# When and in how many issues q is asked for in a fused attention and feed-forward kernel

## The chip, the cores and the metric

The kernel runs on one core of a Trainium2 chip. The metric is the device time of one execution in microseconds (us), lower is better. Engines are called PE (TensorE, matrix products), DVE (VectorE), ACT (ScalarE), POOL (GpSimd) and SP (SyncE, which here only issues DMAs). A DMA is issued by an engine's queue (in this kernel SP's, POOL's and, at the start and the end, ACT's).

## The reference

```python
# q, k, v: (8, 8, 576, 64)   batch, heads, sequence, head size
kv  = np.einsum('bhsd,bhse->bhde', k, v)
out = np.einsum('bhsd,bhde->bhse', q, kv)
rms = np.sqrt(np.mean(out * out, axis=-1, keepdims=True) + 1e-06)
attn = out / rms * g_norm
# (B,H,S,D) -> (B*S, H*D) = (4608, 512)
x = attn.transpose(0, 2, 1, 3).reshape(B * S, H * D)
h = x @ w_in                     # (512, 2048)
r = np.maximum(h, 0.0)
y = (s * (r * r) + b) @ w_out    # (2048, 512)
```

All data is float32; the changes of this study touch only how q is brought into the chip.

## The kernel before

The 4608 rows of x are cut into 36 chunks of 128 rows, and four chunks make a unit: nine units. For each unit the kernel computes attention of its four chunks, then the first product (x @ w_in), the squared relu, and the second product (@ w_out). The attention of unit u + 1 is laid beside the products of unit u, two chunks at a time, so that PE goes from one product to the next. The large products are done in the manner of Strassen (seven products in place of eight, with sums on DVE); names such as x1, z2, x6, y7, x5, x3, y4 are the seven partial products, and the letter is the PSUM tag they use.

The order on each engine is the order in which the program calls its functions (`tc.manual_schedule()`); waits on semaphores are added where one instruction needs another's data or buffer.

**How q comes in.** `load_q(c)` (L132) fills one tile q_sb of 128 x 1024 for chunks c and c + 1. The pool has two buffers (`qp`, L77), so the tile of chunk 8 takes the buffer of chunk 4, and its DMAs wait until the last reader of that one is done (`norm`, L559). From chunk 4 on the tile is put together from pieces: `parts` (L119) says which columns j of which batch a chunk has, and for each piece of n neighbouring columns there are 16 DMAs, one for each of 8 heads and 2 halves of 32 in the head. Chunks 4 and 5 have two single columns (n = 1) and one piece of 6; chunks 6 and 7 one piece of 8; chunks 8 and 9 two pieces of 4; chunks 10 and 11 one piece of 8. `loads(u, i)` (L1599) issues them all on POOL's queue; i is the half of the unit. At most eight DMAs of POOL are under way at a time: each issue waits for the one eight before it.

**What reads q.** `attention_of_two(c)` (L490) gives the steps, in this order: `turn` (DVE transpose, L514, into qT), `product` (PE, L526, into y_ps), `back` (DVE, L538), `square` (ACT, L545), `row_sum` (L549, L553), `norm` (DVE, L557 and L559), `turn_x` (DVE, L570), `scale` (ACT, L488). A is the first pair of chunks of the next unit, B the second. These steps are hung into the products by tables: `side_of` (L1571) for the second product of the first two units, by slot number, and `sides` (L1665) for the first product of later ones.

**The first unit.** It runs beside the conversion of the weights, which come as raw tiles of 1 MB (`load_w`, L177, on SP's queue, three buffers): each is worked over by ACT (`raw`, L217 and L222) and DVE (`convert`, L227 and L237), and then the next raw tile is asked for. `first_unit` (L1613) interleaves this with the plain first product, in slots n. When g_s1(0), a DVE sum, is done, POOL is let on by a tiny copy called begin, and asks for q of the second unit, chunks 4 to 7.

**The stores.** In the second product of unit 0 (`mm2(0)`) the partial products x3 (slots 10 and 11) and y4 (slots 12 and 13) each end with `store` (L1187): two DMAs on POOL's queue. The steps of `side_of` for slot n follow the product of slot n. After the last slot the second unit (u = 1) starts; it asks for chunks 8 to 11 first of all, and then for its weights by SP (`pump`, L1009; the ring w_sb).

Of the kernel before, what the change touches and what calls it, by code (L numbers as in the profile page):

```python
# [16 lines left out]
def kernel(  # L17
# [39 lines left out]
    nc = tc.nc  # L57
    P = 128
    B, H, S, D = q.shape
# [59 lines left out]
    def parts(c):  # L119

        if c < 4:
            return [(0, c, 1), (0, 4 + c, 1)]
        if c == 4:
            return [(0, 8, 1), (0, 17, 1), (1, 0, 2)]
        g, i = divmod(c, R)
        if g == 0:
            return [(1, 4 * i - 18, 4)]
        if i == 4:
            return [(2 * g, 16, 2), (2 * g + 1, 0, 2)]
        return [(2 * g, 4 * i, 4)] if i < 4 else [(2 * g + 1, 4 * i - 18, 4)]  # L130

    def load_q(c, queues=(nc.sync, nc.sync), rest_on=nc.gpsimd):  # L132

        t = qp.tile([P, 2 * DM], FP32, name="q_sb", tag="q")
        q_tile[c] = t
        if c < 4:
            for i in range(2):
                q_in[c + i] = t[:, i * DM : i * DM + DM].rearrange("p (h d) -> p h d", h=H)  # L140
            for s, queue in enumerate(queues):
                for i in range(2):
                    b, j, _ = parts(c + i)[s]
                    queue.dma_start(
                        out=q_in[c + i][s * HB : s * HB + HB],
                        in_=q[b].rearrange("h (p j) d -> p j h d", j=R)[:, j],
                    )
            return []
        pieces, w = [], 0
        for b, j, n in parts(c) + parts(c + 1):  # L150
            if pieces and pieces[-1][1] == b and pieces[-1][2] + pieces[-1][3] == j:
                pieces[-1][3] += n
            else:
                pieces.append([w, b, j, n])
            w += n
        rest = []
        for w, b, j, n in pieces:
            src = q[b].rearrange("h (t j) d -> h t j d", j=JC)
            to = t.rearrange("p (a w d) -> p a w d", a=NP, d=32)
            for h in range(H):  # L160
                for a in range(2):
                    rows = slice(32 * (2 * (h % 2) + a), 32 * (2 * (h % 2) + a) + 32)
                    rest.append(
                        partial(
                            rest_on.dma_start,
                            out=to[rows, h // 2, w : w + n, :],
                            in_=src[h, :, j : j + n, a * 32 : a * 32 + 32],
                        )
                    )
        return rest  # L170
# [152 lines left out]
    for h in range(H):  # L323
        e = D // KC
        nc.gpsimd.dma_start(
            out=g_col[h * e : h * e + e, :], in_=g_norm.rearrange("(e c) -> e c", c=KC)
# [282 lines left out]
    ga, g_pair = {}, {}  # L609
# [901 lines left out]
    turn, take, product, square, root, norm, turn_x = zip(*(attention(c) for c in range(4)))  # L1511
# [59 lines left out]
    def side_of(A, B, sums, u):  # L1571

        if u == 0:
            return {
                6: [A["turn"], lambda: kv_product(1)],
                8: [A["product"], A["back"], A["square"]],
                9: [A["row_sum"], B["turn"]],
                10: [A["norm"], A["turn_x"], A["scale"], B["product"], B["back"], B["square"]],
                11: [B["row_sum"], B["norm"]],
                12: [B["turn_x"], B["scale"], lambda: [fn() for fn in sums_w_in(0)]],  # L1580
                13: [sums],
            }
        of_w_in = [
            partial(sums_of_w_in, *with_tags)
            for with_tags in zip(DEEP, ((5, 6), (7, 4), (5, 6)))
        ]
        return {
            0: [A["scale"]],
            1: [B["turn"]],
            4: [B["product"], B["back"], B["square"]],  # L1590
            5: [B["row_sum"]],
            6: [B["norm"], of_w_in[1]],
            8: [B["turn_x"], B["scale"], of_w_in[2]],
            11: [sums],
            13: [partial(loads, 3, 1)],
            3: [of_w_in[0]],
        }

    def loads(u, i):  # L1599

        if u < U:
            for load in load_q(4 * u + 2 * i):
                load()  # L1603
# [9 lines left out]
    def first_unit():  # L1613
        of_x = x_sums(0)
        of_w = []

        for n, slot in enumerate(slots0):
            if n == 11:
                of_w[1]()
            if n > 1:  # L1620
                out_of = slot()
                if out_of:
                    out_of()
                if n % 4 == 0:
                    g_s1(n // 4 - 1)
                if n == 4:
                    t = small("begin", 1)
                    nc.gpsimd.tensor_copy(out=t, in_=ga["s1", 0][:, 0, :1])
                    loads(1, 0)
                    loads(1, 1)  # L1630
            if 0 < n < 9:
                raw(n + 2)
                convert(n + 2)
            elif n == 0:
                continue
            elif n == 9:
                of_w += sums_w_in(3)
                of_w[0]()
            elif n == 10:
                of_x[0]()  # L1640
                raw(11)
                of_x[1]()
            if n < 11:
                scale_g()
            if n == 9:
                more(8)
        a = mm1(0, NS - 1)
        for fn in (
            a["x1"], scale_g, partial(convert, 11), partial(more, 9),
            a["z2"],  # L1650
            a["x6"], partial(raw, 12), scale_g, partial(g_s1, 2),
            a["y7"], partial(convert, 12),
            a["x5"], partial(raw, 13), scale_g, partial(more, 10), partial(more, 11),
        ):
            fn()
        return a
# [71 lines left out]
    for u in range(U):  # L1728
        A, B = pairs_of(u + 1) if u + 1 < U else (None, None)
        if u == 0:  # L1730
            last = first_unit()
            second = mm2(0)
        else:
            if u == 1:
                loads(2, 0)
                loads(2, 1)
            first, at_second = sides(u, A, B)
            if u > 1:
                run, last = mm1_deep(u)
                second = mm2(u, last, at_second)  # L1740
                run(lambda n: [fn() for fn in first.get(n, [])], second["early"])
                second["rest"]()
                continue
            steps = [mm1(u, s) for s in range(NS)]
            second = mm2(u)
        for s in range(NS if u > 0 else 0):
            a = steps[s]

            def at(n):
                for fn in first.get((s, n), []):  # L1750
                    fn()

            at(0)
            a["x1"]()
            if s:
                x3(steps[s - 1])
            a["z2"]()
            at(1)
            if s:
                y4(steps[s - 1])  # L1760
            a["x6"]()
            at(2)
            a["y7"]()
            at(3)
            a["x5"]()
        side = side_of(A, B, lambda: [fn() for fn in x_sums(u + 1)], u)
        for n, slot in enumerate(second):
            slot()
            if u == 0:
                if n == 0:  # L1770
                    convert(13)
                    load_kv(1, 0, convp, tag="raw", bufs=3)
                    for name in ("x3", "y4", "y4_square"):
                        last[name]()
                    raw(14)
                    scale_g()
                    last["x3_s1"]()
                elif n == 1:
                    convert(14)
                    load_kv(1, 1, convp, tag="raw", bufs=3)  # L1780
                    store_w2(1, 5)
                    raw(15)
                elif n == 2:
                    convert(15)
                    t2 = convp.tile([P, 4 * R * D], FP32, name="w_t2", tag="raw", bufs=3)
                    W2_AT[6] = t2[:, : FC // 2 * HN].rearrange("p (f n) -> p f n", n=HN)
                elif n == 4:
                    store_w2(3, 2)
                    sub_w_out(6, 3, 5)
                    store_w2(6)  # L1790
            if n == 0 and u > 0:
                x3(steps[-1])
                y4(steps[-1])
            for step in side.get(n, []):
                step()
        if u == 0:
            tc_late()
            pump()
# [30 lines left out]
```

## Time and profile before

| | |
|---|---|
| median of three plain runs | 911.52 us (911.5, 911.52, 914.25) |
| the profiled execution | 916.24 us, span 914.5 us |
| busy in the span | PE 898.0, DVE 670.1, ACT 355.5, POOL 276.8 us |
| issues of q on POOL (L1603) | 336, 188.3 us |
| issues of stores on POOL (L1191) | 120, 59.3 us |
| first unit's q issues, chunks 4 to 7 | 49.2 to 94.8 us, 64 issues |
| q issues of chunks 8 to 11 | 138.4 to 172.3 us, 48 issues |

The span is the part of the execution that the profile covers; times inside it count from its start. Most of an execution PE is busy, and what the other engines do matters only where PE, or a chain that ends in PE, waits for it. In the lines of a timeline the columns are the start, the duration of the group, the engine, the line of the program, the operation, the tile written and those read, the shape and the number of instructions; in brackets stands how long the engine was idle before the group, and what ended that. In the lines of waits stand the engine and line that waited, what it waited for, the sum in us, how many times, and the longest. The line with PEclk gives the granted clock of PE in 40 slices of the span, 9 for full speed.

### The profile page before, as it was taken

The page shows a single profiled execution, that of the slowest core. Times are in us where ns is not written, and L with a number is a line of the kernel's source. Part 1 is how long each engine was busy: PE and PEld are TensorE (multiplying, and loading weights), DVE is VectorE, ACT ScalarE, POOL GpSimd, SP SyncE. Part 2 cuts the span into 40 slices and gives each one's busy share as a digit, 9 for nine tenths or more (in the row PEclk, how much of TensorE's full clock was granted, in tenths as well). Part 3 has the DMA queues.
Part 4 walks back from the last instruction along what each step waited for, and adds up shares of the span by engine and source line. Part 5 has one row for each costly group of instructions (what it writes and reads, how often), then busy time and mean ns, then how long its engine had stood idle before and what let it go on. Part 6 is the DMA issues. An engine that isn't in the chain of part 4 may idle for free.

```text
span 914.5 us, 19293 instructions
## 1 busy us (share of the span) xinstructions
PE 898.0 (98%) x7494; PEld 824.3 (90%) x7494; DVE 670.1 (73%) x1236; ACT 355.5 (39%) x598; POOL 276.8 (30%) x523
## 2 busy tenths in 40 slices
PE   7999999899999999999999999999999999999998
PEld 6887888788889998999889998999899989999998
DVE  2889686477648886788678858785778768874686
ACT  2878124341146304640276016801581057204710
POOL 2068018303734142830274035603440200021000
PEclk9999999899999999999999999999999999999999
DMA  9686947329953895369725973498539812891286
GB/s 258 214 290 210 315 115 225 92 68 337 382 146 81 248 329 174 74 198 312 249 60 162 296 256 107 112 297 266 142 79 282 299 35 58 268 302 55 58 253 185
DMA packets 117579, 180.35 MB, mean 197 GB/s; under 512 B 25840, under 2 KB 43504, under 8 KB 117488
## 3 DMA queue, kind: packets, MB, share of 16 engines
q1 hardware_dynamic: 96272, 151.68, 53.3%
q0 software_dynamic: 17760, 25.20, 9.6%
q10 hardware_dynamic: 3456, 2.23, 1.0%
q8 instruction: 60, 0.98, 0.4%
q14 instruction: 31, 0.25, 0.1%
HBM read 153.36 MB, written 25.69 MB: 196 GB/s over the span
## 4 chain that ended last, share of the span: by engine, by line
PE 75%; DMA 8%; issue 7%; DVE 6%; POOL 3%; ACT 1%; ACTq 0%; DVEq 0%; POOLq 0%
PE x_ps L91 38%; PE y_ps L91 22%; PE z_ps L91 8%; PE sx_ps L91 4%; DMA q_sb<-in_q_dram 3%; PE y_ps L526 2%; DMA w<-sub 1%; POOL q_sb L1603 1%; DMA out_dram<-o 1%; DMA kv_sb<-in_v_dram 1%; POOL w L1091 1%; DMA w_raw<-in_moe_w_in_dram 1%; DMA w_raw<-in_moe_w_out_dram 1%; PE z_ps L358 1%; DVE xn L559 0%
## 5 line engine op out<-in xcount | busy, mean ns | idle before, releaser
L1603 POOL DMA_DIRECT2D q_sb<-in_q_dram x336 | 188.3, 568 | 143.8 <-ACT a L633 62.9
L1191 POOL DMA_DIRECT2D out_dram<-o x120 | 59.3, 501 | 314.6 <-issue 152.1
L91 PE MATMUL x_ps<-w_sb,sub 128*128 128x128 f32 x1176 | 148.8, 275 | 0.6 <-DVE r L242 0.6
L91 PEld LDWEIGHTS x_ps<-w_sb,sub 128*128 128x128 f32 x1176 | 139.7, 192 | 1.0 <-DVE r L242 0.9
L625 ACT ACTIVATE a<-a,b_col,s_col 128x512 f32<-128x512 f32 x144 | 116.2, 813 | 35.2 <-DVE a L628 28.0
L91 PE MATMUL x_ps<-xs,ws 128*128 128x256 f32 x528 | 125.7, 381 | 2.2 <-ACT r L699 2.2
L91 PE MATMUL y_ps<-xs,wb 128*128 128x256 f32 x528 | 126.4, 385 | 0.4 <-DVE a L242 0.4
L91 PEld LDWEIGHTS y_ps<-xs,wb 128*128 128x128 f32 x528 | 98.6, 192 | 14.1 <-DVE a L242 0.8
L91 PEld LDWEIGHTS x_ps<-xs,ws 128*128 128x128 f32 x528 | 97.0, 191 | 15.2 <-ACT r L699 3.4
L800 ACT COPY a<-x_ps 128x512 f32<-128x512 f32 x28 | 16.4, 584 | 216.2 <-PE x_ps L91 216.0
L91 PE MATMUL x_ps<-xT,wa 128*128 128x256 f32 x360 | 83.7, 381 | 0.1
L91 PEld LDWEIGHTS x_ps<-xT,wa 128*128 128x128 f32 x360 | 66.8, 190 | 10.4 <-issue 1.5
L242 DVE TENSOR_TENSOR r<-sx_ps,a 128x256 f32<-128x256 f32 x63 | 26.6, 422 | 61.7 <-PE sx_ps L91 61.5
L91 PE MATMUL x_ps<-w_sb,a 128*128 128x128 f32 (+1 forms) x432 | 64.9, 298 | 0.0
L91 PE MATMUL y_ps<-w_sb,a 128*128 128x128 f32 (+1 forms) x416 | 62.1, 295 | 0.0
L91 PEld LDWEIGHTS x_ps<-w_sb,a 128*128 128x128 f32 x432 | 58.9, 191 | 3.3 <-issue 0.4
L91 PEld LDWEIGHTS y_ps<-w_sb,a 128*128 128x128 f32 x416 | 56.1, 192 | 2.1
L242 DVE TENSOR_TENSOR a<-y_ps,r 128x512 f32<-128x512 f32 x38 | 26.1, 688 | 39.2 <-PE y_ps L91 31.2
L242 DVE TENSOR_TENSOR r<-x_ps,o 128x256 f32<-128x256 f32 (+1 forms) x84 | 29.7, 354 | 29.3 <-PE x_ps L91 28.6
L91 PE MATMUL y_ps<-w_sb,sub 128*128 128x128 f32 x392 | 49.5, 275 | 0.0
L245 DVE TENSOR_TENSOR a<-a,a 128x512 f32<-128x512 f32 x72 | 46.8, 684 | 0.4
L91 PE MATMUL z_ps<-w_sb,a 128*128 128x128 f32 (+1 forms) x352 | 46.8, 280 | 0.0
(182 smaller groups left out, 1516.0 us busy)
## 6 DMA issues: line engine op xcount, KB each, us to landing
w_sb<-w SPq DMA_DIRECT2D x385, 256.0 KB, 4.6
w_raw<-in_moe_w_in_dram SPq DMA_DIRECT2D x8, 1024.0 KB, 7.4
w_raw<-in_moe_w_out_dram SPq DMA_DIRECT2D x8, 1024.0 KB, 7.4
w_sb<-w SPq DMA_DIRECT2D x14, 512.0 KB, 8.9
w<-sub POOLq DMA_DIRECT2D x28, 256.0 KB, 6.2
out_dram<-o POOLq DMA_DIRECT2D x112, 64.0 KB, 4.0
w_sb<-in_k_dram SPq DMA_DIRECT2D x24, 288.0 KB, 5.0
w_sb<-in_v_dram SPq DMA_DIRECT2D x24, 288.0 KB, 5.3
```

The source lines that it names most:

```text
L91: nc.tensor.matmul(o, lhsT=lhsT, rhs=rhs, start=start, stop=stop, skip_group_check=True)
L242: nc.vector.tensor_tensor(out=o, in0=a, in1=b, op=ALU.add)
L245: nc.vector.tensor_tensor(out=o, in0=a, in1=b, op=ALU.subtract)
L358: nc.tensor.matmul(ps[r][(r ^ l) * HB : (r ^ l) * HB + HB, i, :], lhsT=kv[l][0][rows, j, :], rhs=kv[l][1][rows, j, :], start=(j == 0), sto ...
L526: nc.tensor.matmul(ps[l][32 * p : 32 * p + 32, r, lo:hi], lhsT=bd_kv[b % 2][rows, p, at : at + 32], rhs=st["qT"][rows, p, lo:hi], start=Tr ...
L625: nc.scalar.activation(t, t, AF.Identity, scale=s_col, bias=b_col)
L800: nc.scalar.copy(g_tile("a11", s), st["x", s])
L1091: nc.gpsimd.dma_start(out=w3_dram[i][:, m - 4], in_=t)
L1191: queues[s % 2].dma_start(out=view[b, jj, :, cols], in_=st[name, j][s * w : s * w + w, cols])
L1603: load()
```

## The change

Three things are changed. A piece of one single column (n = 1) takes one DMA for four heads in place of four DMAs: h runs over 2 in place of 8, and the DMA's pattern has the four heads h, h + 2, h + 4, h + 6 as a dimension. The copy begin waits for g_s1(1) in place of g_s1(0), and it, with q of the second unit, is put into slot 8 of the first product in place of slot 4. And `loads(2, 0)`, q of chunks 8 and 9, is put into slot 10 of the second product of the first unit, behind A's norm, in place of the start of the second unit; `loads(2, 1)` stays there.

```diff
-            for h in range(H):
+            for h in range(2 if n == 1 else H):
                 for a in range(2):
                     rows = slice(32 * (2 * (h % 2) + a), 32 * (2 * (h % 2) + a) + 32)
+                    d = slice(a * 32, a * 32 + 32)
+                    if n == 1:
+                        rest.append(
+                            partial(
+                                rest_on.dma_start,
+                                out=to[rows, :, w, :],
+                                in_=src[h::2, :, j, d].rearrange("h t d -> t h d"),
+                            )
+                        )
+                        continue
                     rest.append(
...
-                            in_=src[h, :, j : j + n, a * 32 : a * 32 + 32],
+                            in_=src[h, :, j : j + n, d],
...
-                10: [A["norm"], A["turn_x"], A["scale"], B["product"], B["back"], B["square"]],
+                10: [A["norm"], partial(loads, 2, 0), A["turn_x"], A["scale"], B["product"], B["back"], B["square"]],
...
-                if n == 4:
+                if n == 8:
                     t = small("begin", 1)
-                    nc.gpsimd.tensor_copy(out=t, in_=ga["s1", 0][:, 0, :1])
+                    nc.gpsimd.tensor_copy(out=t, in_=ga["s1", 1][:, 0, :1])
                     loads(1, 0)
                     loads(1, 1)
...
             if u == 1:
-                loads(2, 0)
                 loads(2, 1)
```

## The prediction, made before the changed kernel was run

> **What bounds the kernel now.** I read the page first, then the waits of TensorE, then TensorE's timeline around its longest wait, and last POOL's timeline and the DVE instruction that the wait names. From the page:
>
> ```profile
> PE 898.0 (98%) x7494; PEld 824.3 (90%) x7494; DVE 670.1 (73%) x1236; ACT 355.5 (39%) x598; POOL 276.8 (30%) x523
> PEclk9999999899999999999999999999999999999999
> ```
>
> TensorE (PE) is busy for 98% of the span, so a change that adds no matrix work can only win back PE's gaps, or create new ones. The granted clock dips once, in slice 7 (0-based; 160 to 183 us). The waits of PE are few:
>
> ```profile
> PE y_ps L526 <- DVE qT L514: 3.3, 1, 3.3
> PE x_ps L91 <- ACT r L699: 2.2, 2, 1.6
> PE kv_ps L358 <- DMA kv_sb<-in_v_dram: 1.7, 3, 1.0
> ```
>
> The first is one wait of 3.3 us in the second unit; the second is two waits, of 1.57 us (up to 72.14) and 0.62 us (up to 76.47), at the end of the first unit's first product. The third is the start of the kernel, which isn't touched. PE's timeline around the long wait:
>
> ```profile
> 162.21 1.89 PE L91 MATMUL z_ps<-xT,wa 128*128 128x256 f32 x8
> 167.38 1.96 PE L526 MATMUL y_ps<-qT,bd_kv 64*32 64x128 f32 x64 [3.28 <-DVE qT L514]
> 169.27 3.78 PE L91 MATMUL y_ps<-xs,wb 128*128 128x256 f32 x8
> 172.84 2.14 PE L91 MATMUL x_ps<-xs,ws 128*128 128x256 f32 x8
> 174.82 1.89 PE L91 MATMUL y_ps<-xs,wb 128*128 128x256 f32 x8
> ```
>
> Here the reader sees two losses: 3.28 us idle, and then eight matmuls that take 3.78 us where the same eight take 1.89 elsewhere: half clock. What PE waited for, and what POOL (which issues q) did before:
>
> ```profile
> 165.98 1.25 DVE L514 STREAM_TRANSPOSE qT<-q_sb 128x1024 f32<-128x1024 f32 x1 [5.00 <-DMA q_sb<-in_q_dram]
> ...
> 124.51 1.09 POOL L1191 DMA_DIRECT2D out_dram<-o  x2 [29.76 <-DVE inv L557]
> 129.19 1.05 POOL L1191 DMA_DIRECT2D out_dram<-o  x2 [3.58 <-DVE o L242]
> 133.37 1.06 POOL L1191 DMA_DIRECT2D out_dram<-o  x2 [3.13 <-DVE o L242]
> 137.36 1.05 POOL L1191 DMA_DIRECT2D out_dram<-o  x2 [2.93 <-DVE o L242]
> 138.40 3.29 POOL L1603 DMA_DIRECT2D q_sb<-in_q_dram  x6
> ...
> 144.00 3.79 POOL L1603 DMA_DIRECT2D q_sb<-in_q_dram  x7 [0.40 <-DMA out_dram<-o]
> 148.96 11.54 POOL L1603 DMA_DIRECT2D q_sb<-in_q_dram  x21 [1.17 <-DMA q_sb<-in_q_dram]
> ```
>
> DVE stood idle for 5.00 us for q of chunks 8 and 9. POOL could not ask for it before 138.40: the four pairs of stores stand ahead in its queue, and each waits for DVE's sums. The 32nd issue (6 + 1 + 7, then the 18th of the 21) falls at 148.96 + 17 x 0.55 = 158.3 us, and its data lands by 165.98, 7.7 us later, beside four 512 KB loads that SP issued from 155.8 to 157.8.
>
> [...] q's last pieces were slow (7.7 us against a median of 2.7 us for the 32 KB pieces) when SP's loads ran beside them. [...] In the trace POOL's q issues take 0.50 to 1.07 us from 49 to 95 us, where DVE converts weights, and 0.55 to 0.59 from 138 to 172; I keep the slower pace as a bound.
>
> **The change part by part.**
>
> (a) q of chunks 8 and 9 (32 issues) moves from behind all eight stores to behind the first two. These two go at 124.51. The buffer is that of chunks 4 and 5, whose last reader is A's norm on DVE (L559, 124.41 + 1.22 = 125.63), so the first issue comes at about 125.7 instead of 138.4, while SP's queue moves nothing (98 GB/s and a DMA share of 0.40 from 125 to 138). The pace before was (158.3 - 138.4)/32 = 0.62 us with its waits: 125.7 + 32 x 0.62 = 145.5 for the last one. With a landing of 2.7 to 7.7 us q is there at 148 to 153. PE needs the product at 162.21 + 1.73 = 163.94 (the pace of eight such matmuls), the transpose takes 1.25 us, so q is needed by 162.7: some 9 us of cover. The stall goes. What is late next: DVE is free at 160.98 (L628 ends), hence qT at 162.2, and the bd_kv copies end on ACT at 158.1; both are before 163.94, so nothing takes its place.
> Worth: without the stall the matmuls of L526 start at 164.0 and take 1.19 us (the x64 group at 115.39), the next eight 1.83, the next eight 1.73, so the group seen at 174.82 starts at 164.0 + 1.19 + 1.83 + 1.73 = 168.8. That is 6.0 us, of which 3.3 is idle and 2.7 is clock.
>
> (b) Behind the 32 issues: the six later stores (ready at 129, 133, 137) now go at about 145.5 to 148.7 (6 x 0.53). Who waits for them: the output tiles are next written in the second unit's second product, after 200. Then the 16 issues of chunks 10 and 11, from about 149 to 162 with waits on the stores' landing (5.4 us seen), instead of 158.9 to 172.3; their transpose comes beside the product that starts at 190. Cost nothing, the cover is over 30 us. SP is moved past nothing: its ring loads from 139.95 keep their place, and are first read at 190.36.
>
> (c) q of the second unit: POOL's start moves from g_s1(0) (48.5) to g_s1(1) on DVE (63.45 + 0.69 = 64.1). 32 issues of single columns (0.50 us each) become 8 of 32x4x32, a shape whose issues take 0.55 to 0.59 in (a); 16 + 16 others stay. 24 issues at 0.6 to 0.75 end at 79 to 82, all 40 at 88 to 94 (before: 94.8). Their transposes are at 108.17 and 121.81 on DVE: at least 13 us of cover with a 5 us landing.
> What it frees: from 49 to 64 the raw weight tiles fill the DMA engines (share 0.87, 290 GB/s). ACT waits 1.50 us for a raw tile until 59.44, and the chain of waits runs from that landing without a gap through ACT and DVE to PE at 76.47. How much faster the tile would land without q the trace of before doesn't show: tiles asked for before q took 5.9 to 8.3 us, those beside it 7.1 to 7.9. Below: nothing. Above: the two PE waits, 2.2 us. I take 0.4 us, an estimate: the q packets are few bytes (single columns, 4 KB each), and some 5% of a 7.9 us landing. Against it, the later pieces of q now come beside raw tiles 12 to 15; those were in time by 1.4 us or more, and their converts end at 92.6 against PE's use at 95.57.
>
> Sum on the profiled execution's own 916.24 us (span 914.5): -6.0 - 0.4 = 909.8. The three plain runs are 911.5, 911.52 and 914.25; the profiled one is 4.7 above their median. The gap of 2.7 between them is what the half clock costs here, so I read the median as a run with the stall and without the half clock: 911.5 - 3.3 - 0.4 = 907.8.
>
> **The rivals.**
> R1, forecast: the stall goes. R1a (chance 0.45): the median run had only the idle time: 907.8, taken as 907.5 since two PE waits may shrink a little more. R1b (0.28): it had the half clock too: 911.5 - 6.4 = 905.1.
> R2 (0.17), no difference: the stall is peculiar to the profiled execution. For it: 916.24 - 6.0 = 910.2 is already below every plain run. Against it: what holds POOL is the order of its queue, the same in each run. Then only part (c) counts: 910.5 to 911.5.
> R3 (0.10), slower: q of chunk 4 comes late for its transpose, because it is asked for 15 us later and its fused issues are slow. Place: L514 at 108.17. With a landing of 5 us it decides from (103.2 - 64.1)/24 = 1.63 us for an issue; the trace has 1.07 at most[...]. 7 us late costs PE about 5 us (the product is asked for at 115.39, DVE's other work between hides some), and the clock's 2.7: 911.5 - 3.7 + 7.7 = 915.5. That the change does not do what it says is excluded for the order: POOL's order is given by the program, and no other engine's order changes.
>
> **How the numbers follow.** About 0.3%, 2.7 us, is what a measurement of this kernel can tell from no change, so faster means under 908.8. R1a gives that in four cases of five (0.36 of 0.45), R1b always (0.28), R2 hardly (0.02): 0.66. Same: 0.09 + 0.15 = 0.24. Slower: 0.10. The range runs from 903.5 (R1b with more of the 2.2 us from part (c)) to 911.5 (R2's end), leaving out R3 and a few per cent below.
>
> **What would show it.** In the changed profile POOL's first q of chunk 8 is at about 126, the last before 150; L514 near 161 waits for no q; L526's group follows z_ps without a gap and takes about 1.2 us; the PEclk line has no dip; the eight matmuls that took 3.78 take 1.9. Part (c): L217's wait near 59 shrinks from 1.50 to about 1.1, and q of chunks 4 to 7 is issued by 95. Wrong if L526 still waits for qT, if L514 near 108 waits for q, or if the median stays above 910.

## The result, and the profile after

The changed kernel takes 907.33 us in the median of five runs (906.33 to 908.14), against 911.91 us of the kernel before in the same session (five runs, 911.5 to 914.47). The ratio is 0.994, its 95% interval 0.9921 to 0.996: 0.4% to 0.8% faster. The profiled execution took 906.66 us, its span is 904.8 us.

The page of the changed kernel, the granted clock in 40 slices (PE is busy for 893.5 us now, 898.0 before):

```profile
PEclk9999999999999999999999999999999999999999
```

The dip in slice 7 is gone, and the mean granted clock is 1.000, where it was 0.996. The mean is the surer sign of the two: e3 and e4 below ran at 0.998, and 0.2% of their spans is some 1.8 us, under a tenth of one slice of 22.8 us. PE's timeline around the place of the long wait (L536 is L526 of before: the lines behind `load_q` are ten higher in the changed kernel):

```profile
159.42 1.89 PE L91 MATMUL z_ps<-xT,wa 128*128 128x256 f32 x8
161.24 1.16 PE L536 MATMUL y_ps<-qT,bd_kv 64*32 64x128 f32 x64
162.33 1.99 PE L91 MATMUL y_ps<-xs,wb 128*128 128x256 f32 x8
...
165.89 1.89 PE L91 MATMUL y_ps<-xs,wb 128*128 128x256 f32 x8
```

No bracket stands behind L536: it follows its predecessor without a gap, takes 1.16 us where it took 1.96, and the next eight take 1.99 where they took 3.78. From z_ps to the last group shown it is 6.5 us now and was 12.6. The transpose on DVE that PE had waited for, and POOL's queue:

```profile
158.12 1.24 DVE L524 STREAM_TRANSPOSE qT<-q_sb 128x1024 f32<-128x1024 f32 x1
```

```profile
121.73 1.11 POOL L1201 DMA_DIRECT2D out_dram<-o  x2 [33.32 <-DVE inv L567]
123.46 14.64 POOL L1613 DMA_DIRECT2D q_sb<-in_q_dram  x27 [0.62 <-issue]
138.93 1.09 POOL L1613 DMA_DIRECT2D q_sb<-in_q_dram  x2 [0.84 <-DMA q_sb<-in_q_dram]
140.46 0.55 POOL L1613 DMA_DIRECT2D q_sb<-in_q_dram  x1 [0.44 <-DMA q_sb<-in_q_dram]
142.28 1.09 POOL L1613 DMA_DIRECT2D q_sb<-in_q_dram  x2 [1.28 <-DMA q_sb<-in_q_dram]
143.36 3.28 POOL L1201 DMA_DIRECT2D out_dram<-o  x6
```

The 32 issues of chunks 8 and 9 stand between two stores and six, and end 15 us before the transpose, which waits for nothing.

This one execution is 9.7 us shorter in its span, twice the difference of the medians. 6.1 us of it are the long wait and its clock. Some 2.8 us are gained earlier (z_ps stands at 159.42 instead of 162.21): the two short waits of PE for r near 72 and 76 are missing too. Whether the change took those away can only be told by doing its parts one by one.

### The profile page after: what moved, and what is told of

The parts are those of the page before. It is cut to its first block, busy times and chain, and to the rows that moved or that the text cites. A ratio compares the mean times of both kernels' runs of the same rounds, so it can differ in the third digit from the quotient of the medians.

```text
span 904.8 us, 19269 instructions
## 1 busy us (share of the span) xinstructions
PE 893.5 (99%) x7494; PEld 821.4 (91%) x7494; DVE 669.6 (74%) x1236; ACT 355.4 (39%) x598; POOL 265.2 (29%) x499
## 4 chain that ended last, share of the span: by engine, by line
PE 93%; DVE 4%; DMA 1%; ACT 1%; issue 0%; ACTq 0%; DVEq 0%
PE x_ps L91 48%; PE y_ps L91 28%; PE z_ps L91 9%; PE sx_ps L91 4%; PE y_ps L536 2%; DMA kv_sb<-in_v_dram 1%; PE kv_ps L368 1%; PE z_ps L368 1%; DVE xn L569 0%; DVE a L255 0%; PE y_ps L368 0%; DVE sub L255 0%; DVE o L252 0%; DVE xT L580 0%; DVE xs L255 0%
## 5 line engine op out<-in xcount | busy, mean ns | idle before, releaser
L1613 POOL DMA_DIRECT2D q_sb<-in_q_dram x312 | 176.3, 573 | 135.4 <-ACT a L643 62.8
```

## The experiments

**Part (a) alone, and part (c) alone.** The letters are those of the prediction. Two theories stood: that both parts gain, as the profile suggests, or that only the late q of chunks 8 and 9 does, and the short waits differ by chance.

```diff
# e1_move_only, on the kernel before
-                10: [A["norm"], A["turn_x"], ...
+                10: [A["norm"], partial(loads, 2, 0), A["turn_x"], ...
...
-                loads(2, 0)
                 loads(2, 1)
```

> The kernel before with part (a) alone: q of chunks 8 and 9 asked for behind two stores instead of eight; q of the second unit as before. Theory 1 (two independent gains: the late q of chunks 8 and 9, and the raw tiles slowed by the q of the second unit): L526's 3.3 us wait gone and PEclk without a dip, but PE still waits about 2.2 us for r (L699) near 72 and 76; 908.5 us, 3.4 below before and 1 to 2.5 above the changed kernel. Theory 2 (all of it is the late q; that the two short waits were gone in the changed kernel's profile is chance from run to run): 907.3 us, like the changed kernel, and the two short waits differ from run to run.

Measured: 907.53 us (6 runs, 906.35 to 908.42) against 911.52 of before; ratio 0.9954 (0.9937 to 0.9971). That is the changed kernel's time. Among the waits of PE, there is none for qT, while the short ones are still there in this execution:

```profile
PE x_ps L91 <- ACT r L699: 0.9, 2, 0.6
```

```diff
# e2_second_unit_only, on the kernel before: single columns fused as in the change, and
-                if n == 4:
+                if n == 8:
...
-                    nc.gpsimd.tensor_copy(out=t, in_=ga["s1", 0][:, 0, :1])
+                    nc.gpsimd.tensor_copy(out=t, in_=ga["s1", 1][:, 0, :1])
```

> The kernel before with part (c) alone: q of the second unit from slot 8 and single columns fused; q of chunks 8 and 9 asked for behind all stores as before. Theory 1: the two short waits near 72 and 76 are gone, the wait of L526 for qT of 3 to 4 us stays, with half clock in some executions and not in others; 909.5 us, 2.4 below before. Theory 2: 911.9 us, like before.

Measured: 911.32 us (22 runs, 908.62 to 914.63); ratio 1.0002 (0.9991 to 1.0012). No gain is measured: the interval runs from 0.8 us faster to 1.1 slower and leaves out the 2.4 us of theory 1, so theory 2 holds. The waits of PE show the stall, and the short waits as long, to a tenth, as in the run above, although q had been moved away from the raw tiles:

```profile
PE y_ps L536 <- DVE qT L524: 2.4, 1, 2.4
...
PE x_ps L91 <- ACT r L709: 0.9, 2, 0.6
```

```profile
165.28 1.15 PE L536 MATMUL y_ps<-qT,bd_kv 64*32 64x128 f32 x64 [2.36 <-DVE qT L524]
166.35 1.99 PE L91 MATMUL y_ps<-xs,wb 128*128 128x256 f32 x8
```

Here the stall of 2.36 us cost no clock: 1.15 and 1.99 us are the durations at full clock (1.16 and 1.99 in the changed kernel, at a mean clock of 1.000), and the mean clock of this execution is 1.000 too.

**The two halves of part (c).** Later only (the second diff, single columns not fused), and fused only (from slot 4, as before).

> The kernel before with q of the second unit from slot 8, single columns not fused (64 issues). Theory 1a (what counts is that no q lies beside the raw tiles that the first product waits for): as the second-unit-only run within 0.5 us, 909.5; q of chunks 4 to 7 issued until about 106 and chunk 4 still in time for 108. Theory 1b (the number of small issues counts): 911 or more. Theory 2: 911.9.

Measured: 911.53 us (14 runs); ratio 1.0000 (0.9989 to 1.001). The q of chunks 4 to 7 was in time: POOL's last issue of it came at 102.70, and the transposes, at 106.20 for chunks 4 and 5 and at 119.84 for 6 and 7, did not wait.

> The kernel before with single columns in 8 issues instead of 32, from slot 4 as before. Theory 1a: the pieces of 6 and 8 columns now lie beside the raw tiles, so the two short waits stay or grow: 911.5 to 913. Theory 1b (it is the small single-column packets that slow the raw tiles): the waits shrink by half or more, 910.5 or less. Theory 2: 911.9.

Measured: 911.92 us (14 runs); ratio 1.0007 (0.9991 to 1.0023). Neither half does anything that can be measured. The waits of PE in the two, later only and then fused only:

```profile
PE y_ps L526 <- DVE qT L514: 3.2, 1, 3.2
...
PE x_ps L91 <- ACT r L699: 0.6, 1, 0.6
```

```profile
PE y_ps L536 <- DVE qT L524: 2.9, 1, 2.9
...
PE x_ps L91 <- ACT r L709: 0.6, 1, 0.6
```

With q of the second unit from slot 4 the short waits were 2.2 us (before), 0.9 (e1), 0.6 (e4) and, in runs told below, none (e5), 0.5 (e6), 1.8 (e7) and 0.4 (e9); with q from slot 8 they were 0.9 (e2), 0.6 (e3) and none (the changed kernel). The two sets overlap. So do the starts of the group z_ps ahead of L526, which show what was won or lost up to there: 159.87 (e5) to 162.21 us (before) in the first set, 159.42 (the changed kernel) to 161.03 (e2) in the second. The raw tiles asked for between 49 and 59 us landed after 7.1 to 7.9 us before and 4.9 to 5.6 in the changed kernel, but after 5.2 to 6.8 in e1, which has q beside them, and 6.5 and 6.6 in e2, which has not; and the tile asked for at 39.6, ahead of any q, took 8.3 before and 7.1 in the changed kernel. ACT's wait near 59, which the prediction names as a sign, was 1.50 us before and is gone in the changed kernel; but it is gone in e4 too, which has q beside these tiles.

**How late is too late.** q of chunks 8 and 9 in slot 12, behind six stores; and, in the other direction, behind the issues of chunks 10 and 11 as well.

```diff
# e5_behind_six, on the kernel before
-                12: [B["turn_x"], B["scale"], ...
+                12: [B["turn_x"], B["scale"], partial(loads, 2, 0), ...
...
-                loads(2, 0)
                 loads(2, 1)
# e7_q_later, on the kernel before
-                loads(2, 0)
                 loads(2, 1)
+                loads(2, 0)
```

> The kernel before, with q of chunks 8 and 9 in slot 12, behind six stores instead of eight (the changed kernel: behind two). Theory A (all that counts is when this q lands, against some 162.7 us): first issue near 134.5, last near 154, landed by 157 to 162, so the wait of L526 is gone or under 1 us: 907.5 to 908.5. Theory B (the stores' own place, or the idle DMA engines from 125 to 135, are what helps): at least half of the stall stays, 909.5 or more.

Measured: 907.37 us (6 runs); ratio 0.9946 (0.9929 to 0.9962), again the changed kernel's time: theory A. POOL's issues:

```profile
132.08 6.53 POOL L1603 DMA_DIRECT2D q_sb<-in_q_dram  x12
...
147.10 5.45 POOL L1603 DMA_DIRECT2D q_sb<-in_q_dram  x10 [0.71 <-DMA q_sb<-in_q_dram]
```

The last issue ends at 152.55, nine later than in the changed kernel, and still L526 does not wait: its group follows z_ps at 161.69 without a gap and takes 1.16 us. Nor is it the time from 125 to 132 with its lightly used DMA engines (share 0.40 from 125 to 138 in the profile of before) that helps: this q is first asked for at 132.08.

> The kernel before, with the two halves of the third unit's q swapped: chunks 8 and 9 behind all eight stores and behind the 16 issues of chunks 10 and 11. Theory A: q lands 8 to 10 us later than before, L526 waits for qT 11 to 13 us, clock loss as large as seen or a little more: 911.5 + 9 + 1.5 = 922 (920 to 924). Theory B (a later wait elsewhere covers part of it): under 917.

Measured: 922.97 us (4 runs, 922.54 to 924.41); ratio 1.0119 (1.0098 to 1.0139), theory A. PE's timeline and the page's clock (slice 7 at 7):

```profile
175.18 1.96 PE L526 MATMUL y_ps<-qT,bd_kv 64*32 64x128 f32 x64 [11.24 <-DVE qT L514]
177.07 3.31 PE L91 MATMUL y_ps<-xs,wb 128*128 128x256 f32 x8
```

```profile
PEclk9999999799999999999999999999999999999999
```

The stall is 8.0 us longer than in the profile of before, and the kernel is 10.6 us slower (8.9 to 12.7 by the interval): no later wait took any of the delay back. The clock loss after 11.24 us of idle time, (1.96 - 1.16) + (3.31 - 1.99) = 2.1 us, is no larger than in the profile of before after 3.28, where the same two groups lost 2.6 and the third another 0.2. The last section sets the two beside the mean clock.

**Idle time and half clock apart.** Extra matmuls just ahead of L526 let PE work on while q is on its way, into a bank that L526 overwrites.

```diff
# e6_filled (26) and e9_filled_half (13), on the kernel before, attention_of_two
             ps = [ps_t.tile([P, 2, 2 * P], FP32, name="y_ps", tag="t") for _ in range(2)]
+            if c == 8:
+                for _ in range(13):
+                    matmul(ps[0][:, 0, :P], ident, ident, True, True)
```

> The kernel before, with 26 extra 128x128 matmuls (ident by ident, about 2.8 us in all) put on PE just before the products of chunks 8 and 9 (L526), into a bank that these overwrite: PE works on while it would wait for q. Extra work, same results. Theory A (the stall costs idle time of about 3 us plus 0 to 2.7 us of half clock after it): the idle time is spent on the extra matmuls, no half clock in any execution, clock 1.000 in every run, 1 to 1.5 us faster than before: 910.2. Theory B (the half clock is no matter in the median run): 911.5 or, where q came early, more.

Measured: 914.69 us (22 runs), ratio 1.0024 (1.0016 to 1.0033). A miss of mine: I had taken 0.11 us for one of them, and each is two passes. PE's timeline of this run:

```profile
161.62 5.97 PE L91 MATMUL y_ps<-ident 128*128 128x128 f32 x52
```

The filling outlasts the stall by some 3 us, so the time says nothing on the clock, although the mean clock was 0.999 or 1.000 in all 22 runs. Of the 7.4 us above the changed kernel's time the filling is 5.9; the rest isn't explained. The run was repeated with half of the filling.

> As the filled run, with 13 extra matmuls instead of 26: the profile there showed 52 passes of 0.115 us for 26, 5.97 us, so 13 take 3.0 us, about as long as the stall (2.4 to 3.3 us in four profiles). Extra work, same results. Theory A (the half clock adds to the idle time in many executions): PE stays busy or idle for well under 1 us, no half clock, so the time is that without a stall and 3.0 to 3.3 us: 907.4 + 3.2 = 910.6, 1 to 1.5 us below before, and the slowest runs (913 and more) are gone. Theory B (the half clock is no matter in the median run): as before, 911.5 to 912.4.

Measured: 910.6 us (22 runs, 909.17 to 912.33) against 911.96; ratio 0.9987 (0.9978 to 0.9995), all 22 with a mean clock of 0.999 or 1.000. Theory A, to the tenth:

```profile
162.03 3.06 PE L91 MATMUL y_ps<-ident 128*128 128x128 f32 x26
165.02 1.16 PE L529 MATMUL y_ps<-qT,bd_kv 64*32 64x128 f32 x64
166.11 2.00 PE L91 MATMUL y_ps<-xs,wb 128*128 128x256 f32 x8
```

3.0 us of useless work in the gap make the kernel faster, by 0.5 to 2.0 us, because PE comes out of the gap at full clock (1.16 and 2.00 us). The time fits: the runs of before that show no clock loss have a median of 910.5 us (below), so the filling took away the clock loss and left the length of the gap as it was.

**An attempt at a faster version.** With the long wait gone, the short waits are what is left in the middle of the kernel; ACT has raw(11) and a scaling ahead of the copies r.

```diff
# e8_reorder, on the changed kernel, first_unit
-                of_x[0]()
-                raw(11)
-                of_x[1]()
+                of_x[0]()
+                of_x[1]()
...
-            a["x1"], scale_g, partial(convert, 11), partial(more, 9),
+            a["x1"], partial(raw, 11), partial(convert, 11), partial(more, 9),
             a["z2"],
-            a["x6"], partial(raw, 12), scale_g, ...
+            a["x6"], scale_g, partial(raw, 12), scale_g, ...
```

> The changed kernel, and on ACT the copy of x1 (r1, L709) ahead of raw(11) instead of behind it, the copy of x6 (r2) ahead of the scaling that waits for DVE. Theory A (the two short waits of PE near 72 and 76, 0 to 2.2 us by run, come from what stands ahead of these copies in ACT's order): both gone, every run near the fastest of the changed kernel: 906.3, 1 below it. Theory B (they come from DVE being late as a whole): the waits stay as waits for DVE's sums xs or move to the next use of w_up near 78: 907.3 or more.

Measured: 908.7 us (9 runs, 907.0 to 911.52), no faster than the changed kernel and more scattered. Theory B: the waits changed places. The profile is of one of the slower of the nine runs (911.25):

```profile
71.18 1.97 PE L91 MATMUL x_ps<-xs,ws 128*128 128x256 f32 x8 [0.52 <-DVE xs L255]
...
79.57 1.13 PE L91 MATMUL x_ps<-w_up,a 128*128 128x256 f32 x4 [0.30 <-ACT a L635]
```

```profile
PE x_ps L91 <- ACT r L709: 1.4, 1, 1.4
```

The last of these, the longest, ends past 82: a wait for a copy r is still there, only later. Together the three are 2.2 us, as much as the short waits of before.

No version beat the changed kernel; its part (a) alone (e1) and the later place of it (e5) cannot be told from it.

## Why the prediction was right, point by point

**Part (a)'s mechanism and its course.** All as worked out. The pace forecast, 0.62 us an issue, was the pace: (143.36 - 123.46)/32 = 0.62. The transpose waited for no q, nothing took the stall's place, and L536 took 1.16 us for the 1.19 forecast. In the profiled execution the stall was worth 6.1 us for 6.0 forecast.

**Part (b).** Cost nothing, as forecast: the six stores went at 143.36 and the issues of chunks 10 and 11 from 147.84 to 160.4 (forecast 149 to 162), and no wait of PE answers to them.

**Part (c): the term that nothing bears out.** The forecast took 0.4 us out of bounds of 0 and 2.2. The interval of e2, 0.8 us faster to 1.1 slower, excludes the upper end and cannot tell 0.4 from nothing. The step that failed was to tie the short waits to q beside the raw tiles: the runs show these waits coming and going whether q is there or not. What makes the raw tiles land sooner in one run than in the next was not tried. The order of events in (c) was right (40 issues from 62.35 to 88.40, chunks 4 to 7 in time): R3 found no ground.

**The median run and the half clock.** This reading failed. I took a median run of before for one with the stall and no half clock, an estimate from the 2.7 us between the three plain runs. Over 99 runs of the kernel before in these sessions the median is 911.93 us, and the mean clock sorts them: 42 runs at 0.999 or 1.000 have a median of 910.5, 42 at 0.997 or 0.998 have 912.4, and 15 at 0.996 have 913.6. The three kernels without the stall and without filling (the changed one, e1 and e5, 17 runs) have 907.3. So the stall alone costs 3.2 us, and in 57 runs of 99 a clock loss of 1.9 or 3.1 comes on top. In the 70 runs of all kernels without the stall (these and e6, e8, e9) the mean clock was below 0.999 once.

The profiles say the same. In the four with the late q in its place of before (before, e2, e3, e4) the stall is 3.28, 2.36, 3.22 and 2.95 us, in the mean 3.0; the clock cost 2.8, 0, 1.5 and 1.6 us, in the mean 1.5. Together 4.4 us, against 4.0 measured for (a) alone and 4.6 for the change. The forecast of 3.3 + 0.4 = 3.7 (taken as 907.5 us, where 907.33 was measured) came near because the missing clock and the gain of (c) that wasn't there nearly cancel: the mechanism of (a) was understood, but how near the number came is luck.

**The rivals.** R2, that the stall belongs to the profiled execution, is refuted by the profiles of e2, e3 and e4, which all show it. R1 came true, with a truth between its two cases: some runs of before had the half clock and some had not.

## What to carry to other kernels

Here a transfer was as late as its queue made it: look at what stands ahead of the issue that a stalled engine waits for, and move only that; 32 issues past six stores were the whole gain, and both places tried that land q before its use, behind two stores and behind six, give the same time. One profile's short waits on a chain that is late as a whole are no basis for a term of the sum: change the suspect alone and time it, since they may differ from run to run. Where PE stalls for about 3 us, as in this kernel, count a clock loss beside the idle time, as a mean over runs rather than as there or not: here it came to 0, 1.9 or 3.1 us between the medians of the three groups of runs.

## What the runs showed of the hardware that was not expected

The same stall cost clock in one run and none in the next: of the 22 runs of e2, all of one kernel, nine have a mean clock of 0.999 or 1.000 and thirteen one of 0.996 to 0.998. The profile of before, cut where its granted clock changes (in each line the stretch, its length, the busy time and instructions of PE, PEld, DVE, ACT and POOL, the granted clock, then the share and GB/s of the DMA engines):

```profile
160.00:166.51 6.51, 4.10 (x19) 3.25 (x18) 1.48 (x3) 3.32 (x5) 2.17 (x4) 1.00 0.88 265
166.51:173.33 6.82, 5.96 (x74) 4.79 (x75) 2.23 (x4) 0.81 (x1) 5.80 (x11) 0.50 0.27 57
173.33:180.00 6.67, 6.67 (x33) 5.87 (x31) 4.53 (x8) 2.92 (x4) 0.00 (x0) 1.00 0.00 0
```

The half clock begins at 166.51, 2.4 us into the stall, and ends at 173.33. Of its 6.82 us PE was idle for 0.87; the other 5.95 cost the three groups of matmuls 2.8 us, about half. In e4 the first group after the stall took 1.54 us, between the 1.16 of full clock and the 1.96 of before, so there the clock probably fell only after PE had gone on working (an estimate from these three durations).

The five profiles with a stall, by its length. The clock not granted is 1 less the mean clock, times the span; since the mean has three decimals, it is an estimate to some 0.5 us. The clock loss is what the groups after the stall took above their durations at full clock:

| profile | stall, us | mean clock | clock not granted, us | clock loss, us |
|---|---|---|---|---|
| e2 | 2.36 | 1.000 | 0 | 0 |
| e4 | 2.95 | 0.998 | 1.8 | 1.6 |
| e3 | 3.22 | 0.998 | 1.8 | 1.5 |
| before | 3.28 | 0.996 | 3.7 | 2.8 |
| e7 | 11.24 | 0.992 | 7.4 | 2.1 |

The loss does not grow with the stall: e7 has the most clock not granted, 7.4 us, but its groups lost only 2.1, so most of the half clock probably fell into its idle time (an estimate from the same two numbers). The means of 0.998 and 0.996 are those of the groups of 42 and 15 runs above, and the losses of 1.5, 1.6 and 2.8 us stand beside the 1.9 and 3.1 between the medians. What decides whether a run loses clock, and how much, the runs do not show.

In the profiles without the stall the groups at this place ran at full clock: 1.16 us for the group of L526 and 1.99 or 2.00 for the next in the changed kernel, e1, e5, e6, e8 and e9. And 3 us of throwaway matmuls in such a gap were worth 0.5 to 2.0 us.
